# Where two reloads and two second-stage loads stand at the end of a convolution loop

## The chip, the core and the metric

The kernel runs on one core of a Trainium2 chip. The metric is the device time of one execution in microseconds (us). A profile of one execution stands beside the timed runs; all its times count from the start of the profiled span.

## The reference, cut to what matters

The result mixes two branches row by row with a learned gate.

```python
x = A_u                                             # 1 x 2048 x 512
g = sigmoid((x * gate_w).sum(-1, keepdims=True))    # one gate per row
a = irfft(rfft(pad(u)) * rfft(pad(K)))[:L] + u*Dskip  # long convolution, K from the SSM parameters
b = gelu(x @ w1 + b1) @ w2 + b2                     # 512 -> 1792 -> 512
return g * a + (1 - g) * b
```

The convolution of 2048 points per channel is done as a two-stage transform: 32 columns `n` of 64 points each, a product of signal and taps in the transformed domain, an inverse first stage per column, and an inverse second stage that mixes the 32 columns.

## The kernel before, in words

The program has two parts. `front` (to about 400 us) computes the dense branch, the taps and the first stage of the signal transform; a planner with a table of due times sets its order, and it writes the dense branch `b` into the output tensor `out` in DRAM. `conv` follows and is written out by hand under a manual schedule: each engine runs its instructions in the order in which the Python code issues them.

`conv` has a loop of 16 steps `s`, two columns `n` per step. In step `s` DVE multiplies signal and taps (`product`), PE transforms the signal of step `s+1` (`signal`) and the taps of step `s+2` (`taps`), PE does the inverse first stage (`inverse`, tile `pa`), and `turn` copies its two results on ACT into one of six `sa` buffers (L1313) and stores each, 256 KB, from the SP queue into the DRAM tensor `t4_d` (L1315; the profile calls it `t_d`). So a pair of buffers is used again three steps later.

After every eighth column one group `g` of 8 columns is complete in DRAM, and `turn` loads it back with rows and columns exchanged (L1330): four loads of 512 KB, one into `den` (output rows of `m` = 0, 1) and three into `t3` (the profile's `t`: `m` = 2, 3, then 4, 5, then 6, 7). Groups 0, 1 and 2 are loaded from the POOL queue. Some of their loads have to wait until other data has left `t3`; these go to the list `held`, and the loop takes them from it, one per step, at L1397 to L1399. Group 3, which is complete only after the last step, is loaded from the ACT queue, its `den` part as two loads of 256 KB.

`dense(k)` reloads the dense branch of output pair `k`, 512 KB, from `out` into SBUF (`attic`, or `loft` for the last three), and `gated(k)` multiplies it with its gate on ACT. `TIMES` names the loop steps at whose end the eight reloads stand, in the order `HERE` then `THERE`.

After the loop PE does the matmuls that `front` left over (`rest`, tile `acc`, L1360 to L1362). Then comes the inverse second stage (L1426, tile `pb`): eight pairs `m` in the order `ORDER` = 0, 1, 2, 3, 6, 7, 4, 5, called k = 0 to 7 here. Each reads 4 of the 32 slots in `den` and `t3`, which all four groups have filled, DVE (L1442), or ACT and POOL (L1439, L1440), add it to the reloaded dense branch, and SP stores 512 KB to `out` (L1446; the last pair in three pieces, L1435 and L1444).

A DMA takes part in two orders. It is issued in the order of its queue's engine (SP, ACT or POOL), and it uses one of eight lanes (semaphores DMAHW0 to 7 for SP and ACT, DMASW0 to 7 for POOL); a DMA waits at issue for the landing of the one before it on its lane. A lane that stands among an instruction's waits in a list below can also mean the data that it brings.

Of the kernel before, what the change touches and what calls it, by code (L numbers as in the profile page):

```python
# [89 lines left out]
N_ATTIC, N_LOFT, N_TK = 11, 8, 10  # L90
ASIDE = (4, 6, 13, 14)
ORDER = (0, 1, 2, 3, 6, 7, 4, 5)
TIMES = (5, 6, 7, 8, 10, 12, 13, 14)
HERE, THERE = (7, 6, 0, 1, 2, 3), (4, 5)
N_DEN = 8
N_ROOM = N_ATTIC + N_LOFT
# [311 lines left out]
def gated_mix(  # L408
# [18 lines left out]
    nc = tc.nc  # L427
# [790 lines left out]
    def conv(pool, ps, late, attic, loft, den, shed):  # L1218
# [11 lines left out]
        def consts(m):  # L1230
            cc = pool.tile([P, 384], F32, tag="cc", name=f"cc{m}", bufs=4)
            nc.sync.dma_start(cc, c2[m])
            c4s[m] = cc

        def fetch(n):
            if 16 <= n < 24:
                t2s[n] = t3[:, n]
            else:
                t2s[n] = pool.tile([P, D], F32, tag="tk", name=f"tk{n}", bufs=N_TK)
            nc.sync.dma_start(t2s[n], tk_d[ko[n]])  # L1240

        def matrices(m):

            cc = c4s[m]
            f = cc[:, 0:256].rearrange("p (n k) -> p n k", n=4)
            f1 = f1s[m % 2]
            for a in (0, 64):
                re, im = slice(a, a + 32), slice(a + 32, a + 64)
                if m < 2:
                    nc.gpsimd.tensor_scalar(f1[re], f[im], -1.0, None, ALU.mult)  # L1250
                    nc.gpsimd.tensor_copy(f1[im], f[re])
                else:
                    nc.scalar.mul(f1[re], f[im], -1.0)
                    nc.scalar.copy(f1[im], f[re])
            mats[m] = (f, f1), cc[:, 256:384].rearrange("p (s k) -> p s k", s=2)
# [23 lines left out]
        def signal(s):  # L1279
            pus[s] = []  # L1280
            for c in range(2):
                pu = ps.tile([P, D], F32, tag=f"pu{2 * (s % 2) + c}", name=f"p2u{s}{c}", bufs=1)
                pair(s, 0, c, pu)
                pus[s].append(pu)

        def product(s):

            (ur, ui), (kr, ki) = pus.pop(s), fac.pop(s)
            v = [vs[2 * i + s % 2] for i in range(2)]
            nc.vector.tensor_mul(v[0], ur, kr)  # L1290
            nc.vector.tensor_mul(v[1], ur, ki)
            nc.vector.tensor_mul(zs[0], ui, ki)
            nc.vector.tensor_mul(zs[1], ui, kr)
            nc.vector.tensor_sub(v[0], v[0], zs[0])
            nc.vector.tensor_add(v[1], v[1], zs[1])
            prod[s] = v
# [36 lines left out]
        held = []  # L1333

        def dense(k, on):

            q = (*HERE, *THERE).index(k)
            if q < 5:
                mos[k] = attic[:, 2 * q : 2 * q + 2]
            else:  # L1340
                r = 2 * q - 10
                mos[k] = loft[:, r * D : (r + 2) * D].rearrange("p (s d) -> p s d", s=2)
            on.dma_start(mos[k], out[2 * k : 2 * k + 2].rearrange("s p d -> p s d"))

        def gated(k):

            for i in range(2):
                z = mos[k][:, i]
                nc.scalar.mul(z, z, gate[:, 1, 2 * k + i : 2 * k + i + 1])

        def rest(n):

            while late and n:
                s, h, l, w, wl = late.pop(0)
                first = s not in accs
                last = not any(e[0] == s for e in late)
                if first:
                    accs[s] = ps.tile([P, D], F32, tag=f"pu{s}" if s > 1 else f"pk{s}", name=f"acc{s}", bufs=1)
                ss = slice(s % 2 * P, s % 2 * P + P)
                nc.tensor.matmul(accs[s], h[:, ss], w, start=first, stop=False)  # L1360
                nc.tensor.matmul(accs[s], h[:, ss], wl, start=False, stop=False)
                nc.tensor.matmul(accs[s], l[:, ss], w, start=False, stop=last)  # L1362
                n -= 1
# [16 lines left out]
        for s in range(16):  # L1380

            for n in range(2 * s + N_TK + (2 if s else 0), 2 * s + N_TK + 4):
                if n < 24:
                    fetch(n if n < 16 else n + 8)
            if s == 0:
                for n in range(16, 24):
                    fetch(n)
            if s in (2, 4, 6, 8):
                consts(s // 2 + 3)
            if s % 2 and s < 13:  # L1390
                matrices(s // 2 + 2)
            product(s)
            if 0 < s < 15:
                signal(s + 1)
            if s + 2 < 16:
                taps(s + 2)
            if s in (9, 10, 13, 14):  # L1397
                to, rows = held.pop(0)
                nc.gpsimd.dma_start(to, rows)  # L1399
            if s == 15:  # L1400
                rest(N_REST)
            inverse(s)
            turn(s)
            if s in TIMES:
                dense((*HERE, *THERE)[TIMES.index(s)], nc.sync)
            if s > 9:
                gated(HERE[s - 10])
        rest(18)

        for s in range(4):  # L1410
# [122 lines left out]
```

## Time and profile before

| what | value |
|---|---|
| median of 3 runs | 504.18 us (502.92 to 505.89) |
| the profiled execution | 504.54 us |
| its span | 502.8 us, so 1.74 us lie around it |
| mean granted TensorE clock | 0.984 |
| busy, share of the span | PE 97%, DVE 85%, ACT 71%, POOL 14% |
| `front` | up to about 400.5 us |
| loop | about 400.6 to 467.8 us (issue of its last store) |
| `rest` on PE | ends at 477.0 us |
| inverse second stage on PE | 481.25 to 497.79 us |

The busy share is an average over stages with different limits, so the stage that the change touches has to be read by itself: the chain of waits for what ended last, the order of instructions in time for who stood still, and a table of 5 us windows for the granted clock and the rate of the DMA engines. In that table the last three columns are the granted clock of PE, the mean busy share of the 16 DMA engines (packets in flight can make it exceed 1) and the GB/s moved.

### The profile page before, as it was taken

How to read it: one execution, taken by the hardware profiler on the slowest of the kernel's cores; microseconds unless marked ns; L12 is line 12 of the kernel's file. 1: busy time of each engine (PE TensorE's matmuls, PEld its weight loads, DVE VectorE, ACT ScalarE, POOL GpSimd, SP SyncE). 2: the span in 40 equal slices, each digit the busy share in tenths (PEclk: the TensorE clock that was granted, in tenths of full speed). 3: DMA queues.
4: the chain of work that ended last, by engine and by line, in shares of the span. 5: the costliest groups of instructions: out<-in, count | busy, mean ns of one | idle time of the engine just before them, and what ended most of it. 6: DMA issues, size and time to landing. Idle time of an engine off the chain costs nothing.

```text
span 502.8 us, 12225 instructions
## 1 busy us (share of the span) xinstructions
PE 485.5 (97%) x4798; PEld 377.9 (75%) x4798; DVE 426.9 (85%) x793; ACT 356.5 (71%) x647; POOL 71.4 (14%) x115
## 2 busy tenths in 40 slices
PE   6999999999999999999999999999999989999976
PEld 5998898898898888989879888988988822223622
DVE  6999999999999999998999999999820269999234
ACT  4999768799884969977587996576533657889113
POOL 1012022101020101201221110011020040121003
PEclk8899999999999999999999999999999999999978
DMA  8977999955789625988973558795557999999867
GB/s 288 389 196 184 300 251 245 304 156 147 162 260 225 170 85 109 273 214 207 261 188 44 189 87 190 181 312 158 181 186 169 258 346 393 354 412 367 332 236 265
DMA packets 85001, 116.58 MB, mean 232 GB/s; under 512 B 39900, under 2 KB 41456, under 8 KB 84400
## 3 DMA queue, kind: packets, MB, share of 16 engines
q1 hardware_dynamic: 74880, 86.54, 53.5%
q0 software_dynamic: 9680, 27.04, 24.3%
q10 hardware_dynamic: 384, 2.23, 1.3%
q8 instruction: 37, 0.61, 0.5%
q14 instruction: 20, 0.16, 0.1%
HBM read 65.97 MB, written 49.81 MB: 230 GB/s over the span
## 4 chain that ended last, share of the span: by engine, by line
PE 60%; DVE 15%; DMA 9%; ACT 8%; issue 4%; SPq 3%; POOL 1%; DVEq 0%; ACTq 0%
PE pk L831 7%; PE ph L1023 7%; PE ph L1025 7%; PE ph L1024 6%; PE acc L1068 6%; PE p2k L1268 6%; PE acc L1069 5%; PE acc L1070 5%; PE pb L1426 3%; PE pa L1307 3%; DVE y L794 3%; DVE y L806 2%; PE p2u L1268 2%; DMA t_d<-sa 2%; PE ph L537 2%
## 5 line engine op out<-in xcount | busy, mean ns | idle before, releaser
L1023 PE MATMUL ph<-xh,wh 128*128 128x256 f32 x448 | 129.0, 288 | 3.1 <-ACT wh L932 3.0
L1025 PE MATMUL ph<-xh,wl 128*128 128x256 f32 x448 | 127.9, 286 | 0.9 <-DVE wl L934 0.9
L1024 PE MATMUL ph<-xlo,wh 128*128 128x256 f32 x448 | 127.7, 285 | 0.0
L1023 PEld LDWEIGHTS ph<-xh,wh 128*128 128x128 f32 x448 | 86.2, 192 | 9.5 <-issue 3.8
L1024 PEld LDWEIGHTS ph<-xlo,wh 128*128 128x128 f32 x448 | 86.3, 193 | 2.0
L1025 PEld LDWEIGHTS ph<-xh,wl 128*128 128x128 f32 x448 | 86.2, 192 | 1.4 <-DVE wl L934 1.4
L1068 PE MATMUL acc<-wh,hh 128*128 128x512 f32 x206 | 83.0, 403 | 0.0
L1069 PE MATMUL acc<-wl,hh 128*128 128x512 f32 x206 | 81.0, 393 | 0.0
L1070 PE MATMUL acc<-wh,hl 128*128 128x512 f32 x206 | 80.5, 391 | 0.0
L1040 ACT ACTIVATE ph<-ph,b1t 128x256 f32<-128x256 f32 x112 | 50.6, 452 | 32.4 <-PE ph L1025 30.5
L831 PE MATMUL pk<-y,den 128*32 128x64 f32 x2048 | 61.6, 290 | 0.1
L831 PEld LDWEIGHTS pk<-y,den 128*32 128x32 f32 x2048 | 57.2, 136 | 3.8 <-issue 2.1
L1053 DVE TENSOR_TENSOR hl<-ph,hh 128x512 fp32r<-128x512 f32 (+1 forms) x62 | 38.5, 622 | 24.3 <-ACT hh L1043 21.4
L1068 PEld LDWEIGHTS acc<-wh,hh 128*128 128x128 f32 x206 | 38.7, 188 | 18.6 <-issue 8.8
L794 DVE TENSOR_TENSOR y<-y,ea 128x64 f32<-128x64 f32 (+4 forms) x80 | 45.6, 570 | 1.4 <-ACT y L784 1.0
L1070 PEld LDWEIGHTS acc<-wh,hl 128*128 128x128 f32 x206 | 38.7, 188 | 8.7
L1069 PEld LDWEIGHTS acc<-wl,hh 128*128 128x128 f32 x206 | 38.7, 188 | 6.0
L1043 ACT CAST hh<-ph 128x512 fp32r<-128x512 f32 (+1 forms) x62 | 33.1, 533 | 13.7 <-PE acc L1069 11.9
L637 DVE TENSOR_TENSOR loft<-den,zz 128x256 f32<-128x256 f32 (+2 forms) x48 | 37.5, 780 | 0.2
L638 DVE TENSOR_TENSOR loft<-den,zz 128x256 f32<-128x256 f32 (+2 forms) x48 | 37.4, 779 | 0.1
L806 DVE TENSOR_TENSOR y<-y,loft 128x2048 f32<-128x2048 f32 x16 | 36.7, 2292 | 0.6 <-ACT loft L755 0.5
L1098 POOL DMA_DIRECT2D out_dram<-b2b x16 | 14.3, 913 | 100.8 <-DMA out_dram<-io 99.3
(188 smaller groups left out, 889.9 us busy)
## 6 DMA issues: line engine op xcount, KB each, us to landing
tu_d<-attic SPq DMA_DIRECT2D x64, 128.0 KB, 4.8
tk_d<-sk SPq DMA_DIRECT2D x32, 256.0 KB, 5.2
t_d<-sa SPq DMA_DIRECT2D x32, 256.0 KB, 5.7
tk<-tk_d SPq DMA_DIRECT2D x24, 256.0 KB, 5.0
t<-t_d POOLq DMA_DIRECT2D x9, 512.0 KB, 7.5
attic<-in_xt_dram SPq DMA_DIRECT2D x16, 256.0 KB, 5.2
xh_d<-xh SPq DMA_DIRECT2D x8, 512.0 KB, 5.9
xl_d<-xlo SPq DMA_DIRECT2D x8, 512.0 KB, 7.1
```

The costliest lines, as they stand in the source:

```text
L794: nc.vector.tensor_mul(both(n, 64 - 3 * n, n), both(0, 64 - n, n), an)
L806: v.tensor_mul(y[:, 0].rearrange("p (a b) c -> p a b c", a=2), e.rearrange("p (a b) c -> p a b c", a=2), cc,)
L831: nc.tensor.matmul(pks[q][32 * j : 32 * j + 32, :, gg], x[:, r, :, ch], y[:, r, :, ch], start=(r == 0), stop=(r == 1), skip_group_check=True,)
L1023: nc.tensor.matmul(p, h, xh[xk][:, d], start=(d == 0), stop=False)
L1024: nc.tensor.matmul(p, h, xlo[xk][:, d], start=False, stop=False)
L1025: nc.tensor.matmul(p, lo, xh[xk][:, d], start=False, stop=(d == 3))
L1040: nc.scalar.activation(phs[q][:, n], phs[q][:, n], AF.Gelu_apprx_tanh, bias=b1t[:, f : f + 1])
L1053: nc.vector.tensor_sub(lo, phs[q][:, 0:nf], hi.bitcast(F32))
L1068: nc.tensor.matmul(a, h, wh[1][w], start=start, stop=False)
L1069: nc.tensor.matmul(a, h, wl[1][w], start=False, stop=False)
L1070: nc.tensor.matmul(a, l, wh[1][w], start=False, stop=(j == 3))
L1268: nc.tensor.matmul(out[64 * i : 64 * i + 64], w, x, start=True, stop=True)
```

## The change

Three things change, all in `conv`. The six reloads of `HERE` are issued at the end of steps 4, 5, 6, 7, 8 and 10 (before: 5, 6, 7, 8, 10, 12). The two of `THERE` leave the loop (before: steps 13 and 14). The two held loads of group 2 (512 KB each) leave the loop too (before: POOL at steps 13 and 14). These four are issued after the loop's last stores: the one for `m` = 6, 7 and `dense(4)` on SP, the one for `m` = 4, 5 and `dense(5)` on ACT.

```diff
-TIMES = (5, 6, 7, 8, 10, 12, 13, 14)
+TIMES = (4, 5, 6, 7, 8, 10)
 HERE, THERE = (7, 6, 0, 1, 2, 3), (4, 5)
...
-            if s in (9, 10, 13, 14):
+            if s in (9, 10):
                 to, rows = held.pop(0)
                 nc.gpsimd.dma_start(to, rows)
...
             inverse(s)
             turn(s)
             if s in TIMES:
-                dense((*HERE, *THERE)[TIMES.index(s)], nc.sync)
+                dense(HERE[TIMES.index(s)], nc.sync)
             if s > 9:
                 gated(HERE[s - 10])
+        for (to, rows), on, k in zip(held[::-1], (nc.sync, nc.scalar), THERE):
+            on.dma_start(to, rows)
+            dense(k, on)
         rest(18)
```

Three lines are added, so lines after L1408 carry a number higher by three or so afterwards (L1426 becomes L1429).

The end of the SP queue, from the stores of step 12 or 13 to the first store of results. `t_d<-sa` is a store of the loop, `loft<-out_dram` a reload. Before:

```order
L1343 DMA loft<-out_dram 128x2x512
L1315 DMA t_d<-sa_4825 64x2x512
L1315 DMA t_d<-sa_4826 64x2x512
L1343 DMA loft<-out_dram 128x2x512
L1315 DMA t_d<-sa_4827 64x2x512
L1315 DMA t_d<-sa_4828 64x2x512
L1343 DMA loft<-out_dram 128x2x512
L1315 DMA t_d<-sa_4823 64x2x512
L1315 DMA t_d<-sa_4824 64x2x512
L1446 DMA out_dram<-attic 128x2x512 x3
```

Now:

```order
L1315 DMA t_d<-sa_4825 64x2x512
L1315 DMA t_d<-sa_4826 64x2x512
L1315 DMA t_d<-sa_4827 64x2x512
L1315 DMA t_d<-sa_4828 64x2x512
L1315 DMA t_d<-sa_4823 64x2x512
L1315 DMA t_d<-sa_4824 64x2x512
L1409 DMA t_4799<-t_d 32x4096
L1343 DMA loft<-out_dram 128x2x512
L1449 DMA out_dram<-attic 128x2x512 x3
```

The three reloads that stood among the stores of steps 12 to 15 are gone from there (one is now at step 10), and one load of group 2 and one reload stand behind the last store.

The end of the ACT queue, from the last step's loads of group 3 on, with the semaphores that each instruction waits for. Before:

```order
L1330 DMA den<-t_d 32x2048
L1330 DMA t_4799<-t_d 32x4096 [waits DMAHW1_49,DMASW6_49,DMASW5_49]
L1330 DMA t_4799<-t_d 32x4096 [waits DMAHW4_49]
L1330 DMA t_4799<-t_d 32x4096
L1349 ACTIVATE loft<-loft,gate 128x512 x2
L1439 ACTIVATE sa_4823<-pb_5503,gate 128x512 [waits PE_49,Activation_49]
```

Now:

```order
L1330 DMA den<-t_d 32x2048
L1330 DMA t_4799<-t_d 32x4096 [waits DMASW6_49,DMASW5_49]
L1330 DMA t_4799<-t_d 32x4096
L1330 DMA t_4799<-t_d 32x4096 [waits DMAHW5_49]
L1349 ACTIVATE loft<-loft,gate 128x512 x2
L1409 DMA t_4799<-t_d 32x4096 [waits DMAHW6_49]
L1343 DMA loft<-out_dram 128x2x512 [waits DMAHW7_49]
L1442 ACTIVATE sa_4823<-pb_5503,gate 128x512 [waits PE_49,Activation_49]
```

Two DMAs stand in front of the first `sa<-pb` product now. By the order in which lanes are given out, lane 5 holds the load that SP issues at L1409, lane 6 the first and lane 7 the second `den` load of group 3, so ACT waits for these three landings before it goes on.

The end of the POOL queue, one piece of the difference:

```order
 L1330 DMA den<-t_d 32x4096
 L1330 DMA t_4799<-t_d 32x4096
-L1399 DMA t_4799<-t_d 32x4096 x2
-L1440 TENSOR_TENSOR attic<-attic,sa_4823 128x512
-L1440 TENSOR_TENSOR loft<-loft,sa_4824 128x512
...
+L1443 TENSOR_TENSOR attic<-attic,sa_4823 128x512
+L1443 TENSOR_TENSOR loft<-loft,sa_4824 128x512
```

POOL loses the two held loads of group 2 and has nothing to issue after the first two loads of that group.

## The prediction

> **What bounds the kernel now.** I read three views, each for the stage behind the loop. First the chain of waits that ended last (start, length, what), its last part:
>
> ```profile
> span 502.8 us, 12225 instructions
> ```
>
> ```profile
> 467.84 10.12 DMA t_d<-sa
> ...
> 478.13 2.98 DMA den<-t_d
> 481.12 0.14 issue
> 481.25 16.54 PE pb L1426 x68
> ```
>
> The last store of the loop is issued at 467.84 and needs 10.12 us to land; only then can ACT issue the first `den` load of group 3, which needs 2.98 us; only then does the second stage start. Next, PE in order of time (in brackets: idle time before it, and what ended that):
>
> ```profile
> 476.60 0.39 PE L1362 MATMUL acc<-wh,hl 128*128 128x512 f32 x1
> 481.25 6.22 PE L1426 MATMUL pb<-den,g1t 128*64 128x512 f32 x16 [4.26 <-DMA den<-t_d]
> 487.29 10.49 PE L1426 MATMUL pb<-t,g1t 128*64 128x512 f32 x52
> ```
>
> PE covers the chain with `rest` until 477.0, then stands still for 4.26 us. And the 16 matmul records of the first two pairs take 481.25 to 487.29, 6.04 us, where the other 52 (8 of them half as wide, so 48 full ones) take 10.49, or 0.2185 each. Sixteen at that pace are 3.50 us. The windows say why:
>
> ```profile
> 460.00:465.00 5.00, 5.00 (x33) 2.49 (x25) 4.94 (x9) 5.00 (x10) 2.10 (x4) 1.00 0.99 313
> 465.00:470.00 5.00, 5.00 (x25) 3.31 (x24) 0.86 (x2) 1.43 (x3) 0.00 (x0) 1.00 1.02 378
> 470.00:475.00 5.00, 5.00 (x23) 4.13 (x22) 0.99 (x2) 0.00 (x0) 0.00 (x0) 1.00 0.95 362
> 475.00:480.00 5.00, 1.99 (x9) 1.31 (x7) 1.56 (x3) 0.00 (x0) 0.00 (x0) 0.96 0.38 127
> 480.00:485.00 5.00, 3.75 (x10) 1.38 (x12) 0.78 (x2) 1.33 (x2) 0.00 (x0) 0.50 0.97 341
> 485.00:490.00 5.00, 5.00 (x22) 1.67 (x20) 2.94 (x4) 0.69 (x1) 0.74 (x1) 0.85 0.54 212
> ```
>
> The granted clock is 0.50 after the standstill. So late data costs twice: 4.26 us of waiting, and 6.04 - 3.50 = 2.54 us of half clock. The DMA engines are full (share 0.95 to 1.02) from 460 to 475 and nearly idle while ACT waits. The 10.12 us are therefore a queue, and its content can be counted.
>
> **The change part by part.** What stands ahead of the last store (start, time to issue, queue):
>
> ```profile
> 459.63 0.48 SPq L1343 DMA_DIRECT2D loft<-out_dram  x1
> ...
> 462.80 0.47 SPq L1343 DMA_DIRECT2D loft<-out_dram  x1
> ...
> 465.42 0.56 SPq L1343 DMA_DIRECT2D loft<-out_dram  x1
> 467.22 1.17 SPq L1315 DMA_DIRECT2D t_d<-sa  x2
> ```
>
> ```profile
> 462.81 1.05 POOL L1399 DMA_DIRECT2D t<-t_d  x2
> ```
>
> Their sizes (issues from 400 us on: count, KB each, median us to landing):
>
> ```profile
> t<-t_d POOLq DMA_DIRECT2D x9, 512.0 KB, 7.5
> loft<-out_dram SPq DMA_DIRECT2D x3, 512.0 KB, 11.3
> ```
>
> *Removed from the queue:* the reloads of 462.80 and 465.42 and the two loads of 462.81, 4 x 512 KB = 2.10 MB; the reload of 459.63 goes to step 10 as well, another 0.52 MB. At (313 + 378 + 362) / 3 = 351 GB/s the 2.10 MB are 6.0 us, all five 7.5 us. The saving has a floor, the latency of a store with little ahead of it, which the stores of step 12 show; the last stores of the loop stand below them:
>
> ```profile
> L1315 SPq DMA_DIRECT2D t_d<-sa x2: 518/536/554, 458.3 to 458.9; - x2
> DMA to landing us min/median/max: 3.3/3.4/3.5
> ```
>
> ```profile
> L1315 SPq DMA_DIRECT2D t_d<-sa x2: 524/538/553, 467.2 to 467.8; - x2
> DMA to landing us min/median/max: 10.1/10.1/10.1
> ```
>
> So the last store lands at 477.96 - 6.0 = 472.0. Bounds: 467.84 + 3.3 = 471.1 below, and 477.96 - 5.0 = 473.0 above (2.10 MB at the fastest window in the loop, 422 GB/s, quoted further down).
>
> *The `den` load.* ACT issues it 0.17 us after the landing, at 472.2. Alone it took 2.98 us. Now SP has put 1.05 MB (the load of group 2 and a reload) behind its last store, and these share the engines with it. If all of it, 1.05 + 0.52 MB, has to pass first from 472.0 - 1.2 on (the bytes are moved before the landing is seen: in the window from 475 the engines worked 0.38 x 5 = 1.9 us, so until 476.9 at the latest, and the landing came at 477.96; I take 1.2), it takes 4.5 us and lands at 476.5. So 475.2 to 476.5, and with the late bound 477.5. `rest` ends at 477.0 whatever happens. PE has no wait, or at most 0.6 us.
>
> On the sharing of engines, the Trainium skill, "DMA: Bandwidth & Descriptors", section on queues, rings and completion order, states that each DMA engine goes round-robin between queues, packet by packet. By that rule ACT's `den` gets half of the engines against SP's two transfers and is done after about twice its own 0.52 MB, an estimate of 3.0 us after its start; that lies inside the two ends above, so the sum does not depend on it. It speaks against the change all the same: SP's new loads no longer delay a store, but a `den` load.
>
> *PE afterwards.* Kind and number of matmuls stay as they are. The change of kind costs 0.32 us from start to start, as it did at step 15:
>
> ```profile
> 464.93 0.39 PE L1362 MATMUL acc<-wh,xlo 128*128 128x512 f32 x1
> 465.25 1.29 PE L1307 MATMUL pa<-v,cc 64*64 64x512 f32 x8
> ```
>
> So from 476.60 the second stage starts at 476.9 instead of 481.25: -4.3 us. Without a standstill the clock stays at 1.00, and pairs k = 0 and 1 take 3.50 instead of 6.04: -2.5 us. Sum -6.8 to -6.9, the end of PE at 476.9 + 3.5 + 10.5 = 490.9. What remains behind it (502.8 - 497.79 = 5.0 us for the last additions and stores) moves along.
>
> *The moved loads in their new place.* ACT's and SP's transfers behind the last store are these and the four moved ones:
>
> ```profile
> 478.13 1.15 ACTq L1330 DMA_DIRECT2D den<-t_d  x2
> 479.40 1.82 ACTq L1330 DMA_DIRECT2D t<-t_d  x3
> ```
>
> That is 2 x 256 KB and 7 x 512 KB, 4.19 MB, from 470.8 at 351 GB/s until 482.7. The load of group 2 for k = 4 stands first on SP and lands near 474; the third load of group 3 is the 3.15 MB point, 479.8 + 1.2 = 481.0, and k = 4 starts at 476.9 + 3.5 + 2 x 1.75 = 483.9 (1.75 = 10.49 / 6 per pair). ACT's load of group 2 is needed at k = 6, 487.4; with the stores of k = 0 and 1 (1.05 MB) all mixed in it lands by 485.4. `dense(5)` has to be there for its gate products at about 488.5; by 486.9. All hidden, with 1.6 us at the closest. If a cover is gone, each us late is one us.
>
> *The last stores.* The old tail, 475 to 505 us in slices of 0.75 us:
>
> ```profile
> DMA  9510026998969834940980988904999999900000
> GB/s 412 208 44 8 0 55 186 350 371 284 350 284 393 350 131 197 369 169 8 366 333 27 380 303 330 366 3 188 374 385 374 391 371 376 329 8 0 0 0 0
> ```
>
> The last bytes moved at 501.2, 1.6 us before the end of the span, at some 378 GB/s; before that the engines often had nothing to do. Now 4.19 MB of loads and eight stores of 512 KB, 8.39 MB in all, run from 470.8. With loads at 351 and stores at 378 they end at 470.8 + 11.9 + 11.1 = 493.8, and the end of the span stays PE's 495.9; with all at the 341 of 480 to 485 they end at 495.4 and the span at 497.0. So 0 to 1.1 us; I take 0.2, since the rate of the stores was seen.
>
> *ACT's new waits.* ACT waits for SP's load of group 2 (about 474) before its third `t` load, and for both `den` landings (by 476.5 to 477.5) before the two new DMAs. Behind them stands the first `sa<-pb` product, which PE makes possible at 476.9 + 3.5 + 0.9 = 481.3. Cost nothing, with 3.8 us of cover.
>
> *Six reloads earlier.* From step 4 to 11 the queue holds 0.52 MB more than before. The loop's DMA windows, the tightest store, and the copy that reuses its buffer:
>
> ```profile
> 435.00:440.00 5.00, 5.00 (x34) 1.48 (x32) 5.00 (x10) 4.09 (x10) 0.00 (x0) 1.00 0.93 348
> ...
> 445.00:450.00 5.00, 5.00 (x40) 1.17 (x31) 5.00 (x9) 3.53 (x8) 2.62 (x5) 1.00 1.10 422
> ```
>
> ```profile
> L1315 SPq DMA_DIRECT2D t_d<-sa x1: 553/553/553, 446.8 to 446.8; - x1
> DMA to landing us min/median/max: 10.4/10.4/10.4
> ```
>
> ```profile
> 457.68 1.08 ACT L1313 COPY sa<-pa 128x512 f32<-128x512 f32 x2
> ```
>
> That store of step 9 lands at 457.2; the copy into the same buffer, the second of the row of 457.68, starts at 458.2. The 0.52 MB cost 1.2 us at 422 and 1.5 at 348 GB/s, minus a little that the 0.93 window takes up. So a stall between 0 and 0.5 us at step 12; I take 0.2. Every other store lands with more room.
>
> **Sum:** -4.3 - 2.5 + 0.2 + 0.2 = -6.4: 504.54 - 6.4 = 498.1 for the profiled execution. That one ran 0.36 us above the median of 504.18, so the median should be **497.8 us**.
>
> **Rivals.**
>
> *A shorter gap stays.* If the last store drains slower or SP's loads hold `den` back, PE stands still for 1 to 2.5 us. What such a gap does to the clock, the trace shows at one place:
>
> ```profile
> 405.77 1.08 PE L1268 MATMUL p2k<-tk,f 128*64 128x512 f32 x4 [1.63 <-POOL f L1251]
> ```
>
> ```profile
> 405.00:410.00 5.00, 4.23 (x20) 1.11 (x20) 2.98 (x6) 2.14 (x4) 3.12 (x6) 1.00 1.10 286
> ```
>
> 1.63 us of idle time left the clock at 1.00, 4.26 us halved it. So 1 to 1.6 us cost only themselves (498.8 to 499.4), and 2.5 us perhaps 2.5 more (502.8); centre 500. For it: shared engines. Against: the 0.4 us or more of cover. The Trainium skill, "TensorE: Matmul & The Clock Gate", Part 1, puts the loss of the clock at an idle window of about 3.4 us; by that rule every gap of this rival costs only itself, and its time is 498.8 to 500.3.
>
> *The loop pays.* If the deeper queue delays the buffers at several steps from 5 to 12, not one, by 0.5 us each over six steps, 3 us go: 500.8. For it: the engines are as good as full there (0.93 to 1.10). Against: the buffers of step 9 are the last ones before their copy by 1.0 us even with POOL's loads beside them, and a store needs 3.4 us without.
>
> *The store's latency is its own.* If what holds the last store is not the transfers ahead but the writing itself, nothing moves: 504.2. Against: 3.4 us at step 12.
>
> *The tail becomes a DMA stage; slower.* In the old tail the rate was 212 GB/s at 485 to 490, with loads and stores mixed. If that is what the engines can do for such a mix, 8.39 MB from 470.8 end at 510.4, the span at 512.0, and the median is 513.4. The change turns slower from below 8.39 / (501.2 - 470.8) = 276 GB/s on. Against: the share was only 0.54 there, so the engines waited for work, and 341 GB/s stood at 0.97.
>
> **How the numbers follow.** Forecast 0.64 (496.8 to 499.0: the bounds of loop and last stores, and `den` early or late by 0.6); shorter gap 0.16; loop 0.06; own latency 0.08; slower tail 0.06. About 0.5%, 2.5 us, is what can be told from no change here. The first three are faster save a tail of the gap and the loop: 0.83. The same 0.11, slower 0.06. The range reaches from 496.0 (no cost in loop and stores, and a spread of the runs of 0.3%) to 502.4, which takes in most of the gap with half clock and the loop.
>
> **What would show it.** Right: last store landing at 471 to 473; no idle time of PE over 1 us before the first `pb` matmul; clock 1.00 through the second stage; PE's end near 491; `sa` copies of step 12 not later than 0.5 us. Wrong: a `pb` matmul that waits for `t` or `den`, a clock of 0.50 behind the loop, or step times over 3.75 us.

## The result, and the profile after

The changed kernel takes 503.45 us (median of 21 executions, 498.89 to 513.85 and one of 1132.76 us). The kernel before, run beside it, takes 505.89 us (median of 21, 502.92 to 510.86). The ratio is 0.9933, 95% interval 0.9912 to 0.9955: 3.4 us faster, between 2.3 and 4.5. All ratios here leave out executions that took over 1.5% longer than the fastest of the same kernel (four of these 21 after, one before). Forecast were 6.4 us, to 497.8 us, and the range ended at 502.4. So the sign is right and the size is not. Some 1.7 us of the distance to 503.45 are the base: the three runs shown before had a median of 504.18, the 21 runs have 505.89. The other 3.9 us belong to the change: 3.0 by the ratio, and 0.9 because the median counts the four long executions too.

The profiled execution after took 501.49 us, with a span of 499.7 us. Its chain of waits (start, length, what):

```profile
447.91 11.84 DMA t_d<-sa
...
471.57 4.07 DMA loft<-out_dram
475.64 3.49 DMA den<-t_d
479.13 0.14 issue
479.26 13.97 PE pb L1429 x68
```

The second stage still hangs on `den`, and `den` still on the loop's last store. The chain names the reload of 471.57, but that one lands only 6.9 us after its issue, at 478.5. What had just landed when ACT could go on was the store, by this row of the stores' line from 468 us on (issue times, then landing):

```profile
L1315 SPq DMA_DIRECT2D t_d<-sa x2: 518/970/1421, 468.7 to 469.3; - x2
DMA to landing us min/median/max: 6.1/6.1/6.1
```

469.33 + 6.13 = 475.46, and ACT issued `den` 0.18 us later. Before, the store took 10.12 us. PE in order of time:

```profile
478.04 0.39 PE L1362 MATMUL acc<-wh,hl 128*128 128x512 f32 x1
479.26 3.65 PE L1429 MATMUL pb<-den,g1t 128*64 128x512 f32 x16 [0.83 <-DMA den<-t_d]
482.72 10.50 PE L1429 MATMUL pb<-t,g1t 128*64 128x512 f32 x52
```

The wait fell from 4.26 to 0.83 us, and the 16 matmuls of the first two pairs take 482.72 - 479.26 = 3.46 us where they took 6.04. The windows (third last column the granted clock, then DMA share and GB/s):

```profile
460.00:465.00 5.00, 4.60 (x31) 1.23 (x27) 4.94 (x9) 5.00 (x10) 0.82 (x2) 1.00 0.84 320
465.00:470.00 5.00, 5.00 (x26) 3.22 (x25) 1.53 (x3) 3.07 (x6) 0.23 (x1) 1.00 0.96 261
470.00:475.00 5.00, 5.00 (x24) 4.14 (x23) 0.75 (x1) 0.00 (x0) 0.00 (x0) 1.00 0.96 318
475.00:480.00 5.00, 4.17 (x20) 2.90 (x20) 2.25 (x3) 1.22 (x2) 0.00 (x0) 1.00 0.88 296
480.00:485.00 5.00, 5.00 (x26) 2.04 (x24) 3.27 (x5) 0.80 (x2) 0.30 (x1) 1.00 0.96 308
485.00:490.00 5.00, 5.00 (x26) 1.94 (x24) 2.16 (x4) 2.41 (x4) 3.37 (x3) 1.00 0.99 380
490.00:495.00 5.00, 3.22 (x20) 1.38 (x16) 3.70 (x6) 2.10 (x4) 1.37 (x2) 1.00 1.05 406
```

The clock stays at 1.00. But the engines, half idle from 475 to 480 and from 485 to 490 before, have a share of 0.88 to 1.05 to the end, and the stores of results show it (issues from 480 us on: count, KB each, median us to landing), first before, then after:

```profile
out_dram<-attic SPq DMA_DIRECT2D x5, 512.0 KB, 3.0
```

```profile
out_dram<-attic SPq DMA_DIRECT2D x5, 512.0 KB, 6.0
```

The loop gained a stall: ACT waits 0.43 us for the store of step 9 before it can use that buffer again at step 12.

```profile
459.82 0.58 ACT L1313 COPY sa<-pa 128x512 f32<-128x512 f32 x1 [0.43 <-DMA t_d<-sa]
```

**Where the time went.** What lies ahead of the loop has the same code in both kernels, but not the same length: the loop's first `pa` matmul starts at 410.45 us before and at 411.58 after, and between 409.05 and 415.70 in the profiles of this study. So lengths are counted below from that matmul. They were read from the start times of the trace, and the columns from "rest ends" to "behind PE" add up to the whole. "Last pa" is the start of the last eight `pa` matmuls, "store" the landing time of the loop's last store, "gap" the time from the end of `rest` (taken as 0.32 us after the start of its last matmul, so a gap is 0.07 us longer here than in the rows of the profile) to the first `pb` matmul, "behind PE" the time from the last `pb` matmul to the end of the span.

| kernel | last pa | store | rest ends | gap | first 16 pb | other 52 | behind PE | whole |
|---|---|---|---|---|---|---|---|---|
| before | 54.80 | 10.1 | 66.46 | 4.33 | 6.04 | 10.49 | 4.97 | 92.30 |
| before, second profile | 54.83 | 9.8 | 66.46 | 4.02 | 5.03 | 10.49 | 4.96 | 90.95 |
| after | 55.34 | 6.1 | 66.78 | 0.90 | 3.46 | 10.50 | 6.50 | 88.13 |
| after, second | 55.04 | 6.4 | 66.50 | 0.85 | 3.45 | 10.50 | 6.89 | 88.20 |
| after, third | 55.39 | 5.3 | 66.86 | 0 | 3.48 | 10.48 | 6.73 | 87.54 |
| after, fourth | 55.86 | 5.2 | 67.32 | 0 | 3.48 | 10.48 | 6.55 | 87.83 |

From the first pair of profiles the change saves 4.2 us (gap -3.4, clock -2.6, loop +0.3, behind PE +1.5). From the means of all six it saves 91.6 - 87.9 = 3.7 us, which agrees with the 3.4 us of the timed runs.

### The profile page after: what moved, and what is told of

Same layout as the page of the kernel before. It is cut to its first block, busy times and chain, and to the rows that moved or that the text cites. A ratio compares the mean times of both kernels' runs of the same rounds, so it can differ in the third digit from the quotient of the medians.

```text
span 499.7 us, 12227 instructions
## 1 busy us (share of the span) xinstructions
PE 483.5 (97%) x4798; PEld 378.1 (76%) x4798; DVE 426.9 (85%) x793; ACT 356.2 (71%) x647; POOL 70.3 (14%) x113
## 4 chain that ended last, share of the span: by engine, by line
PE 79%; DMA 6%; ACT 6%; DVE 5%; issue 2%; POOL 1%; SPq 0%; POOLq 0%; DVEq 0%; ACTq 0%
PE pk L831 11%; PE ph L1023 10%; PE ph L1025 9%; PE ph L1024 9%; PE acc L1068 9%; PE acc L1069 8%; PE acc L1070 8%; PE p2k L1268 4%; PE pb L1429 3%; PE pa L1307 3%; PE ph L537 3%; DMA t_d<-sa 2%; PE p2u L1268 2%; ACT wh L932 1%; DMA sk<-in_w_dram 1%
## 5 line engine op out<-in xcount | busy, mean ns | idle before, releaser
L1043 ACT CAST hh<-ph 128x512 fp32r<-128x512 f32 (+1 forms) x62 | 33.0, 533 | 13.2 <-PE acc L1069 10.1
```

## The experiments

**The change and the kernel before, again.** Three more profiles of the change and one of the kernel before, to see what repeats.

> The changed kernel once more. If the 1.1 us by which the loop began later in its first profile is chance, the loop begins within 1.2 us of 405.8 or 406.9 at random here, and the lengths counted from the loop's start repeat: last store of the loop 6.1 us from issue to landing, 0.8 us of idle time of TensorE before the second stage, clock 1.00, 6.5 us from the end of TensorE to the end of the span. If these lengths differ by over 1 us, a single profile cannot carry terms of that size.

> The change itself, unedited, beside the two kernels above. By its two profiles: last pa matmul 55.0 to 55.4 us from the loop's first, last store 6.1 to 6.4 us, PE's wait for den 0.8 to 0.9 us, tail 6.5 to 6.9, 88.1 to 88.2 us; ratio 0.992 to 0.994. Other lengths would show how far two profiles of one kernel may lie apart.

> The change itself on the same chip as the two above: 0.992 to 0.994 of the time before, 87.5 to 88.2 us from the loop's first matmul, a wait for den of 0 to 0.9 us, a tail of 6.5 to 6.9 us.

> The kernel before, unedited, for a second profile. If the first was typical: last pa matmul 54.8 us from the loop's first, last store landing after 9.5 to 10.5 us, PE's wait 3.8 to 4.8 us, the first 16 pb matmuls 5.5 to 6.1 us (half clock), tail 5.0, 91.5 to 93 us. If it was an execution of the bad kind: a last store of 7 to 8 us, a wait under 2.5 us, full clock, and 88 to 89 us, and then the change's gain in this stage is smaller than the two profiles say.

Ratios of the change: 0.9922 (0.9876 to 0.9967), 0.9932 (0.9894 to 0.997) and 0.9943 (0.9914 to 0.9973). The wait for `den` is there in two of four profiles and gone in the other two, where the store landed in 5.2 and 5.3 us. The kernel before against itself gave 0.9995 (0.9956 to 1.0033). Its second profile has the same wait, but less of the half clock:

```profile
486.18 5.21 PE L1426 MATMUL pb<-den,g1t 128*64 128x512 f32 x16 [3.95 <-DMA den<-t_d]
491.21 9.19 PE L1426 MATMUL pb<-t,g1t 128*64 128x512 f32 x42
```

```profile
480.00:485.00 5.00, 2.23 (x10) 1.50 (x8) 1.80 (x3) 0.00 (x0) 0.00 (x0) 1.00 0.46 150
485.00:490.00 5.00, 3.82 (x12) 1.34 (x14) 1.04 (x2) 1.33 (x2) 0.00 (x0) 0.66 0.94 357
```

The 16 matmuls take 491.21 - 486.18 = 5.03 us. The lost clock costs 1.5 us there and 2.5 in the first profile: it is no constant.

**One half of the change at a time.** `only_held` is the kernel before with the two held loads behind the loop, all eight reloads at their old steps. `only_reloads` is the change with the held loads back on POOL at steps 13 and 14.

```diff
# only_held, against before
-            if s in (9, 10, 13, 14):
+            if s in (9, 10):
...
+        for (to, rows), on in zip(held[::-1], (nc.sync, nc.scalar)):
+            on.dma_start(to, rows)
# only_reloads, against the change
-            if s in (9, 10):
+            if s in (9, 10, 13, 14):
...
-        for (to, rows), on, k in zip(held[::-1], (nc.sync, nc.scalar), THERE):
-            on.dma_start(to, rows)
+        for on, k in zip((nc.sync, nc.scalar), THERE):
             dense(k, on)
```

> The kernel before, with only the two held loads of group 2 moved behind the last stores (one on SP, one on ACT); the eight reloads stay at their old steps. Theory of bytes (the prediction's): what stands ahead counts by its bytes, so this half (1.05 MB) gives half of the saving, the last store takes about 8.1 us (half way from 10.1 to 6.1), TensorE idles 2 to 3 us, ratio to the kernel before 0.995. Theory of packets: POOL's group loads go in 16 KB packets and take the DMA engines from SP's 2 KB packets, so this half gives over two thirds of the saving: store at 7.4 us or less, idle time under 2 us, ratio 0.992 to 0.994.

> The changed kernel, but with the two held loads of group 2 back on POOL at steps 13 and 14; only the reloads are moved. Theory of bytes: half of the saving, the last store takes about 8.1 us, ratio to before 0.995. Theory of packets: less than a third of the saving, the last store takes 8.8 us or more, TensorE idles over 2.5 us, ratio 0.996 to 1.000.

Measured: 0.99 (0.9865 to 0.9935) and 0.9884 (0.9812 to 0.9957). The last store and the start of the second stage, of `only_held`:

```profile
L1315 SPq DMA_DIRECT2D t_d<-sa x2: 524/906/1289, 470.5 to 471.1; - x2
DMA to landing us min/median/max: 7.6/7.6/7.6
```

```profile
482.03 3.65 PE L1428 MATMUL pb<-den,g1t 128*64 128x512 f32 x16 [1.74 <-DMA den<-t_d]
```

and of `only_reloads`:

```profile
L1315 SPq DMA_DIRECT2D t_d<-sa x2: 518/549/580, 466.5 to 467.1; - x2
DMA to landing us min/median/max: 7.3/7.3/7.3
```

```profile
477.67 3.65 PE L1428 MATMUL pb<-den,g1t 128*64 128x512 f32 x16 [1.46 <-DMA den<-t_d]
```

Each half removes 1.05 MB ahead of the store and shortens it by 2.5 to 2.8 us, more than the 2.0 that half of the change's 4.0 would be; neither kind of transfer clearly weighs more. Each half alone also saves the clock (first 16 `pb` matmuls 3.71 and 3.46 us). With only 1.05 MB behind the loop the time behind PE is 5.15 and 5.44 us, not 6.5. Whole lengths: 87.65 and 88.41 us, against 87.5 to 88.2 for both halves together. So each half by itself brings what the whole change brings: the second half takes the rest of the gap and gives it back behind PE.

**What the last store still waits for.** In `group2_behind` the two loads of group 2 that stay on POOL at step 12 go behind the last store as well, on SP.

```diff
+                    if g == 2:
+                        held2.append((to, rows[:, h:e]))
+                        continue
                     on.dma_start(to, rows[:, h:e])
...
+        for to, rows in held2:
+            nc.sync.dma_start(to, rows)
         for (to, rows), on, k in zip(held[::-1], (nc.sync, nc.scalar), THERE):
```

> The change, with the two loads of group 2 that stayed on POOL at step 12 (1.05 MB) issued on SP behind the loop's last store too, ahead of the third. Nothing but stores is then in the queues when the last two stores are issued. Theory 1 (what the last store waits for is these two loads): it lands 3.3 to 3.7 us after its issue, as a store with little ahead of it did in the trace of before, against 6.1. Theory 2 (a store at this place has its own 5 to 6 us, whatever is beside it): 5 us or more. In both the first pb matmul now waits for POOL's former loads as well, 1.05 MB issued at the end of the loop: they land 5 to 8 us later, so PE waits 1 to 3 us, and the length from the loop's first matmul is 88 to 91 us (88.13 for the change).

```profile
L1315 SPq DMA_DIRECT2D t_d<-sa x2: 518/536/553, 471.7 to 472.3; - x2
DMA to landing us min/median/max: 2.4/2.4/2.4
```

```profile
481.34 3.65 PE L1434 MATMUL pb<-den,g1t 128*64 128x512 f32 x16
```

The store needs 2.44 us and PE does not wait at all. So POOL's two loads are what keeps it at 5.2 to 6.4 us in the change. All bytes together: 9.8 to 10.1 us with 3.15 MB ahead, 7.3 to 7.6 with 2.10, 5.2 to 6.4 with 1.05 in the change (4.7 to 7.4 over all kernels here with these 1.05 MB), 2.4 with none. So more bytes mean a later landing, but 1.05 and 2.10 MB overlap. The expected wait of 1 to 3 us did not come: the new SP loads hold back ACT's two `den` loads (median 6.4 us here, 3.0 in the trace of before), but these land just within the cover. Whole length 87.17 us, ratio 0.9909 (0.9872 to 0.9947); ACT's stall at step 12 was 1.05 us in this execution.

**Packet size.** In `thin_after` each 2 KB row of the scratch is followed by 2 KB of nothing, so that group loads no longer come in 16 KB pieces (by the packets of its trace, POOL's come in 4 KB, those of SP and ACT in 2 KB).

```diff
-    t4_d = dr.tile([4, 2, GROUP, 2, 32, D], F32, name="t4_d")
+    t4_d = dr.tile([4, 2, GROUP, 2, 32, 2 * D], F32, name="t4_d")
```

> The change, with each row of the scratch in DRAM (2 KB) followed by 2 KB that nothing uses. Eight rows of a group load are then no longer one run of 16 KB, so its packets become 2 KB like those of a store; bytes and order stay. In the change's trace a group load's packet holds a DMA engine for 0.61 to 1.4 us where a store's packet needs 0.084 us. Theory 1 (the stores behind the loop are late because SP's short packets take turns with POOL's long ones): the stores of the loop land in 3.5 to 6 us throughout, the last one in 3.5 to 5 us rather than 6.1, PE has no wait at step 12 (0.43 before) and none for den (0.83). Theory 2 (bytes alone, or the way the memory is read): the last store keeps 5.8 to 6.5 us, den lands as late as before, and if short packets are read worse, later. A third possibility is that 4 KB from row to row slows the reads as 132 KB from block to block did (pad: last pa matmul 4.6 us later); then both numbers get worse and packet size is not told apart from it.

```profile
L1315 SPq DMA_DIRECT2D t_d<-sa x2: 518/552/587, 468.2 to 468.8; - x2
DMA to landing us min/median/max: 5.5/5.6/5.6
```

5.6 us, within what the change itself shows; ACT stalled 1.2 us in the loop, the whole length is 88.99 us, the ratio 0.9899 (0.986 to 0.9938). Its packets tell more. From 469 to 471 us, with the last two stores of the loop issued and not landed, the DMA engines moved this (queue, packets, MB, share of the engines; q0 is POOL's queue, q1 SP's):

```profile
q0 software_dynamic: 146, 0.54, 93.5%
q1 hardware_dynamic: 8, 0.01, 2.7%
```

In the change, where POOL's packets are 16 KB, from 467.5 to 469.5 us, with the two stores of step 14 issued at 465.3 and 465.9 and landing 8.2 us later:

```profile
q0 software_dynamic: 46, 0.51, 96.7%
```

In both, SP's stores all but stand still while POOL's two loads pass. So long packets are not needed for that; whether the 4 KB from row to row hides a smaller effect is not shown.

**Where the rows lie.** `pad_after` and `pad_before` put two unused rows (4 KB) behind each block of 64 rows.

```diff
-    t4_d = dr.tile([4, 2, GROUP, 2, 32, D], F32, name="t4_d")
+    t4_d = dr.tile([4, 2, GROUP, 66, D], F32, name="t4_d")
...
-                nc.sync.dma_start(t4_d[g, :, k].rearrange("e c q d -> (c q) e d"), sa)
+                nc.sync.dma_start(t4_d[g, :, k, :64].rearrange("e r d -> r e d"), sa)
```

> The change as it is, with one edit: in the scratch in DRAM each matrix's block of 64 rows is followed by two rows that nothing uses, so that blocks lie 132 KB apart rather than 128 KB. Bytes, transfers and their order stay. After the change the last two stores of the loop took 6.1 us to land where the bytes ahead of them made 4.2, and POOL's two loads of group 2 beside them took 7.5 and 8.4 us. Theory 1 (the loads of a group are slow because all their rows lie at a power of two from each other and meet in the memory): POOL's two loads land in 5 to 6.5 us, the last store in 4.2 to 5, and PE waits 0 to 0.3 us for den where it waited 0.83 to 0.90. Theory 2 (the engines are only shared out between the queues, and where the rows lie is nothing to it): 7 to 8.5 us for POOL's loads, 5.8 to 6.5 us for the last store, 0.7 to 1.0 us of waiting; from the loop's first matmul to the end 87.8 to 88.5 us, as before the edit (88.13 and 88.20).

> The kernel before, with the same two rows of padding behind each block of 64 in the scratch. Theory 1 (rows at a power of two): the last store's 10.1 us become 8 or less and PE's 4.26 us become 2 or less, with the clock at 1.00 afterwards; the time falls by 4 us or more. Theory 2 (sharing alone): 9.6 to 10.6 us, 3.8 to 4.8 us, half clock as before, and a time within 1 us of the kernel before.

Measured: 1.006 (1.0023 to 1.0096) and 1.0097 (1.005 to 1.0143). Both are slower than the kernel before, and the loss lies in the loop: the last eight `pa` matmuls start at 59.97 and 59.37 us, some 4.6 us later. ACT's waits within the loop of `pad_after` (in total, times, longest):

```profile
ACT sa L1313 <- DMA t_d<-sa: 5.3, 3, 3.8
```

So it matters to these transfers where the blocks lie, but the old place is the better one. The Trainium skill, "DMA: Bandwidth & Descriptors", section on latency and other measured facts, advises to pad rows that lie at large powers of two by some KB; it measured 512 KB and more. Carried over to 128 KB blocks, which the page did not measure, it would have the padding help; here it hurts.

**Who delays `den`.** In `den_first` all four transfers behind the loop stand on ACT, behind its own loads of group 3.

```diff
-        for (to, rows), on, k in zip(held[::-1], (nc.sync, nc.scalar), THERE):
+        for (to, rows), on, k in zip(held[::-1], (nc.scalar, nc.scalar), THERE):
```

> The change, with all four transfers behind the loop on ACT's queue, behind its own den and t loads of group 3; SP's queue holds nothing behind the last store of the loop. Theory 1 (SP's load of group 2 and its reload share the engines with den, which took 3.49 us rather than the 2.98 of before): den lands in 2.9 to 3.1 us, PE waits 0.3 to 0.5 us rather than 0.83. The load of group 2 for the fifth pair then comes last, 4 us later, and may make a pb matmul wait for up to 1 us. Theory 2 (den is as slow by itself, and what makes PE wait is the store's 6.1 us alone): den 3.4 to 3.6 us, waiting 0.8 to 0.9 us. In both the last store keeps 5.9 to 6.5 us, since what is ahead of it is the same.

```profile
den<-t_d ACTq DMA_DIRECT2D x2, 256.0 KB, 3.0
```

```profile
488.01 3.65 PE L1429 MATMUL pb<-t,g1t 128*64 128x512 f32 x16 [1.26 <-DMA t<-t_d]
492.12 3.66 PE L1429 MATMUL pb<-t,g1t 128*64 128x512 f32 x20 [0.45 <-DMA t<-t_d]
```

Without SP's loads beside it the first `den` load takes 2.9 us, as before; with them 3.0 to 3.5 in the four profiles of the change. So they cost it at most some 0.5 us there. The store itself needed 7.4 us in this execution, with the same queue ahead of it as in the change, so PE waited 1.5 us for `den` all the same. The loads that now come last make PE wait another 1.7 us, the time behind PE is 8.31 us, and the ratio 0.9961 (0.9927 to 0.9995) gives back some 40% of the gain, though its interval overlaps that of the change.

**What lengthens the time behind PE.** `no_tail_reloads` leaves out the two reloads behind the loop, so two pairs are summed with what the buffer held before.

```diff
-            on.dma_start(mos[k], out[2 * k : 2 * k + 2].rearrange("s p d -> p s d"))
+            if on is not None:
+                on.dma_start(mos[k], out[2 * k : 2 * k + 2].rearrange("s p d -> p s d"))
...
-            dense(k, on)
+            dense(k, None)
```

> The change without its two reloads behind the loop (1.05 MB): the dense rows of those two pairs are not read back from DRAM, so the products that use them work on what the buffer holds from before. Theory 1 (the last stores of the kernel come late because the engines have more bytes to move from 470 us on than they can): 1.05 MB at the 390 GB/s of the last stores are 2.7 us less of queue, so the tail behind the last matmul falls from 6.5 to 6.9 us back to the 5.0 us of before, and the length from the loop's first matmul from 88.1 to 86.6 us. Theory 2 (the tail is longer because the second stage's products come closer behind each other at full clock, whatever is read): the tail stays at 6.3 to 6.9 us, the length at 88.1. In both PE's wait for den may fall from 0.85 to 0.3 to 0.6 us, since SP's reload no longer runs beside it.

```profile
out_dram<-attic SPq DMA_DIRECT2D x5, 512.0 KB, 4.4
```

The time behind PE is 5.00 us, as before the change; the last six stores land after 2.8 to 3.4 us. So without the two reloads, 1.05 MB, the 1.5 to 1.9 us are gone. They do not make them alone: in `only_reloads`, with the reloads behind the loop and the held loads not, the time is 5.44 us.

**The steps of the reloads.** `times_back` and `times_back_2` (one kernel, run twice) are the change with its six reloads at their old steps; `best1` adds a seventh at step 13 and leaves only one behind the loop.

```diff
# times_back, times_back_2
-TIMES = (4, 5, 6, 7, 8, 10)
+TIMES = (5, 6, 7, 8, 10, 12)
# best1
-TIMES = (4, 5, 6, 7, 8, 10)
+TIMES = (5, 6, 7, 8, 10, 12, 13)
```

> The changed kernel with the six reloads of the loop back at steps 5, 6, 7, 8, 10 and 12; the four moved transfers stay behind the last stores. If the 0.4 us stall of ScalarE at step 12 comes from the earlier reloads, it is gone here. The reload at step 12 now stands ahead of the last stores: by the theory of bytes 0.52 MB, 1.5 us later landing (7.6 us); if the engines have room at step 12 (they moved 258 GB/s at 462 to 464) it costs nothing. Time within 0.3% of the changed kernel.

> The kernel with the reloads at their old steps (5, 6, 7, 8, 10, 12), run again to tell what the earlier steps cost. If its first profile told the truth: no wait at step 12 (last pa matmul at 54.8 us from the loop's first, against 55.0 to 55.3 for the change), last store 4.9 to 5.5 us, no wait for den, 86.5 to 87.0 us from the loop's first matmul, and 0.985 to 0.990 of the time before. If that was one lucky execution: 6 us for the last store, a wait of 0.5 to 0.9 us, 88 us, and the ratio of the change, 0.993.

> The change with its reloads back at steps 5, 6, 7, 8, 10 and 12, a seventh at step 13 as in the kernel before, and only the eighth behind the loop; the held loads behind the loop as in the change. By the runs so far: with two reloads behind the loop and these steps the last store needed 5.10 us, PE had no wait and the tail was 6.33 us; with none behind it 7.58, 1.81 and 5.15 us. If each reload counts by its bytes, it is in the middle: last store 6.0 to 6.8 us, PE waits 0.5 to 1.2 us at full clock, tail 5.5 to 6.0, and the length from the loop's first matmul 86.7 to 87.4 us, no better than 86.74. If the wait vanishes as long as the last store is under 6 us, 86.0 to 86.5 us, the best of all.

The first profile of `times_back` showed no stall, a store of 5.1 us, no gap and 86.74 us; the second a stall of 0.5 us, a store of 6.1 us, a gap of 1.7 us and 88.13 us. Ratios 0.9899 (0.9822 to 0.9977) and 0.9906 (0.9873 to 0.9939): not told apart from the change. `best1` took 88.43 us from the loop's first matmul, a store of 7.1 us and a gap of 1.3 us, yet its ratio is 1.0029 (0.9989 to 1.0068): its loop began at 415.38 us, 4.9 us later than in the first profile of before. The first loss lies far ahead of the edit, as these windows of `best1` show:

```profile
55.00:60.00 5.00, 3.31 (x16) 1.64 (x11) 1.91 (x6) 4.63 (x9) 0.57 (x1) 0.91 0.97 357
60.00:65.00 5.00, 5.00 (x97) 4.81 (x99) 5.00 (x11) 2.42 (x6) 0.00 (x0) 0.75 0.85 263
```

PE stands still for 0.60 and 1.09 us and then runs at a clock of 0.50 for 3.4 us, 0.75 over the second window; the first profile of before is busy for 5.00 us at 1.00 in both. The instructions there are the same. The three profiles whose loop begins latest, `best1`, `after_4` (414.33) and `before_again` (415.70), all lost the clock at this place, so this is nothing of the edit. Why the executions of `best1` were so long as a whole stays open.

**Both causes taken away.** `best2` (run twice) has the reloads at their old steps and all loads of group 2 behind the loop; `best3` has all eight reloads in the loop too.

```diff
# best2, against group2_behind
-TIMES = (4, 5, 6, 7, 8, 10)
+TIMES = (5, 6, 7, 8, 10, 12)
# best3, against group2_behind
-TIMES = (4, 5, 6, 7, 8, 10)
+TIMES = (5, 6, 7, 8, 10, 12, 13, 14)
...
-                dense(HERE[TIMES.index(s)], nc.sync)
+                dense((*HERE, *THERE)[TIMES.index(s)], nc.sync)
...
-            dense(k, on)
```

> The change with both suspected causes taken away: its six reloads back at steps 5, 6, 7, 8, 10 and 12, and POOL's two loads of group 2 issued on SP behind the loop's last store. If these two are the whole of what was missing in the middle of the chain: last pa matmul at 54.8 us from the loop's first, last store landing after 2.4 to 3.5 us, no wait for den, tail 5.8 to 6.5 us, so 86.0 to 86.8 us from the loop's first matmul (before 92.3, the change 88.1) and 0.985 to 0.989 of the time before, faster than the change by 1.5 to 2 us. If the delay in the loop was chance and has nothing to do with the steps, 87.0 to 87.4 us, as group2_behind, and no difference from the change that the runs can tell.

> The change with the reloads at their old steps and all four loads of group 2 behind the loop, a second time. If its first result holds: 0.985 to 0.990 of the time before, 86.0 to 86.6 us from the loop's first matmul, no wait for den. If it was chance: 0.992 to 0.994, as the change, with a delay in the loop of 0.5 to 1 us.

> All eight reloads at their steps of the kernel before (5 to 14), and all four loads of group 2 behind the loop's last store. Two reloads (1.05 MB) then stand ahead of the last stores, and nothing of the dense part behind them. From the runs so far: last pa matmul 54.8 us from the loop's first; the last store has the reload of step 14 and no group load ahead of it, 3.5 to 4.5 us; den lands within the cover, no wait; the tail returns to the 5.0 us of before. So 85.4 to 85.9 us from the loop's first matmul and 0.983 to 0.988 of the time before, the best of all. Against it: if a store needs 6 us or more with a reload ahead, PE waits 0.5 to 1 us, and 86.5 us is no better than best2.

`best2`: 0.9877 (0.9831 to 0.9922) and 0.9876 (0.9825 to 0.9927), medians 500.37 and 499.38 us, beside 501.81 and 502.92 us for the change on the same chips. Over both chips the mean of its 12 executions is 500.24 us, that of the change's 24 is 502.77; the difference of 2.5 us has a standard error of 0.6, from their scatter of 1.6 and 2.0 us. So `best2` is faster than both kernels. Its stores and its second stage, first profile:

```profile
L1315 SPq DMA_DIRECT2D t_d<-sa x2: 518/536/553, 469.5 to 470.1; - x2
DMA to landing us min/median/max: 2.4/2.4/2.4
```

```profile
479.16 3.65 PE L1434 MATMUL pb<-den,g1t 128*64 128x512 f32 x16
482.64 10.47 PE L1434 MATMUL pb<-t,g1t 128*64 128x512 f32 x52
```

| kernel | last pa | store | rest ends | gap | first 16 pb | other 52 | behind PE | whole |
|---|---|---|---|---|---|---|---|---|
| best2 | 54.81 | 2.4 | 66.44 | 0 | 3.48 | 10.47 | 5.91 | 86.30 |
| best2, second | 54.81 | 2.4 | 66.44 | 0.47 | 3.45 | 10.50 | 6.71 | 87.58 |

The first profile is 6.0 us shorter than the first of before, nearly the forecast. In the second `den`, now beside 2.1 MB of SP's loads, came 0.4 us late, and the time behind PE was 0.8 us longer: 87.58, outside what was expected. `best3`: 0.988 (0.9822 to 0.9938), store 4.7 us, a stall of 0.9 us in the loop, a gap of 1.1 us, 5.27 us behind PE, 87.81 us. It is no better: what it saves behind PE it pays in front.

All in all a stall of ACT for a `t_d` store stands in each of the nine profiles with the reloads at steps 4 to 10 (0.2 to 1.2 us, the padded ones not counted), and in two of nine with the old steps (0.5 and 0.9).

## Why the prediction was right and wrong

*Right in mechanism.* The second stage waited for the last store, and that store for bytes ahead of it. The rival that its latency is its own fell with `group2_behind`: 2.44 us. Without a long gap ahead of it the second stage has a clock of 1.00, and in the change and `best2` the 16 matmuls take 3.45 to 3.48 us as forecast (3.50). Gaps of 0.40 to 1.92 us (the longest in `pad_after`) left them at 3.45 to 3.71, gaps from 3.95 us on (3.95, 4.26, 6.37) stretched them to 4.84 to 6.04. The Trainium skill, "TensorE: Matmul & The Clock Gate", Part 1, puts the bound at an idle window of about 3.4 us; these gaps agree, but other places in the traces do not. In the loop of `pad_before` a wait of 2.09 us was enough for 3.41 us at half clock:

```profile
463.73 1.56 PE L1307 MATMUL pa<-v,cc 64*64 64x512 f32 x8 [2.09 <-ACT sa L1313]
```

```profile
465.81:469.22 3.41, 3.41 (x12) 2.28 (x14) 0.00 (x0) 2.13 (x4) 1.95 (x4) 0.50 1.06 405
```

And at 59 us, far ahead of the loop, two waits close together did it in three profiles: 0.60 and 1.09 us in `best1`, 1.18 and 1.09 in `after_4`, 1.54 and 1.09 in `before_again`. So the length of one gap does not decide it, and the bound stays open; that gaps of 0.8 us ahead of the second stage keep the clock is what the profiles of the change show. The forecast term of -2.5 us was read from one execution; by the second profile of before it is -1.5.

*The last store: 2.10 MB are not 6.0 us.* This term failed: it was put at 6.0 us and measured 4.0. The forecast divided the removed bytes by 351 GB/s, as if the engines went on at that rate without them. They did not. From 460 to 475 the windows give (313 + 378 + 362) x 5 = 5.27 MB before and (320 + 261 + 318) x 5 = 4.50 MB after. The missing 0.77 MB are 2.2 us at 351 GB/s, and 6.0 - 2.2 = 3.8; measured were 10.12 - 6.13 = 4.0. (With the windows of after shifted by the 1.1 us by which its loop began later, it is 4.43 MB, and 3.6.) A part of the fall is an empty queue (share 0.84 at 460 to 465), a part a low rate at a full share (261 GB/s at 0.96), while POOL's two loads pass and SP's stores stand still. The other three profiles of the change have 285, 279 and 245 GB/s from 465 to 470. So what is left ahead weighs more than its bytes at 351 GB/s. Why POOL's loads move so slowly, and why SP's queue stops beside them, stays open: 16 KB packets (`thin_after`) were not needed for it, and padding made the transfers slower. The bounds of 471.1 to 473.0 for the landing missed 475.46, and 474.3 with the later start of the loop taken off. The floor, 3.3 us from step 12, was too high too: with nothing beside it a store lands in 2.4.

*The `den` load.* Its own time was right: 3.5 us after the landing, between the 3.0 and 4.3 (472.2 to 475.2 and 476.5) that were said; 3.0 to 3.5 over the four profiles, and 4.3 in `times_back_2` with the same transfers beside it. It was late because the store was. The Trainium skill, "DMA: Bandwidth & Descriptors", section on queues, rings and completion order, lets the queues take turns; the estimate by it was 3.0 us, which is also what `den` takes with nothing beside it, so the change does not test the rule. `group2_behind` and `best2` do, with more left to move on SP's queue, and no turns show: by the packets of their traces, `den`'s first came 3.9 to 4.0 us after its issue, while SP's queue moved 1.26 to 1.33 MB, where it comes after 1.3 us with nothing beside it. That is the forecast's other end, by which what was issued earlier passes first.

*The gap.* Forecast 0 to 0.6 us; it was 0.83 in the first profile of the change, 0.8 in the second, none in two others. That lies between the forecast and the rival of the shorter gap (1 to 2.5 us), and by that rival's cause: the store drained slower.

*The last stores: +0.2 us were +1.5 to +1.9.* This is the other failed term, above its bound of 1.1. The loads went at 296 to 318 GB/s from 470 to 485, not at 351: 4.19 MB take 13.7 us at 306, 1.8 more than the forecast's 11.9, and the stores queue behind them. `no_tail_reloads` shows that the difference goes with the two reloads. In part this is the rival of a tail that becomes a DMA stage: the engines are the bound behind PE, without turning the change slower.

*The loop.* Forecast +0.2 us (0 to 0.5); the last eight `pa` matmuls start 0.2 to 1.1 us later in four profiles, mean 0.6 and in three of them above the bound, by one stall at step 12 and not by several steps.

Put together, from the first pair of profiles: -6.4 forecast, +0.9 gap, +1.3 behind PE, +0.1 loop, so -4.1 where -4.2 was measured; 1.1 us of that went again because the loop began later in that execution, which is nothing of the change.

## What to carry to other kernels

Bytes taken out of a full queue are worth their time only as long as the queue stays full and keeps its rate: read the windows for what else would run short, and look for what remains ahead of the transfer that counts. Here that was 1.05 MB on another engine's queue; moving it as well, with the reloads at their old steps, gave the one kernel (`best2`) that the runs show to be faster than the change. Bytes that are moved behind a stage come back at its end, so before moving all of them, test how many are needed to close the gap: each half of this change closed enough of it to keep the clock, and brought as much as the whole.

## What was not expected of the hardware

- A store of 256 KB lands in 2.44 us with nothing beside it, and in 4.7 to 7.4 us with the same 1.05 MB ahead of it, in executions of kernels that differ only behind it.
- While POOL's two loads pass, SP's queue moves next to nothing for 2 us (0.51 MB against none), though two of its stores are issued. Loads that come in 4 KB packets or in 16 KB packets delay the stores alike (5.6 against 5.2 to 6.4 us), while 4 KB of padding every 128 KB lengthens the loop by 4.6 us.
- Unchanged code ahead of the loop ends between 409.05 and 415.70 us from execution to execution, a spread larger than the effect that was to be measured. In the three latest, two waits of PE close together, of 0.60 to 1.54 us, were followed by 3.4 to 6.8 us at half clock.
